# GroupNorm with 4 MiB tiles: the last store of each run issued in four gated quarters of 32 rows

## The chip, the core and the metric

The kernel runs on one core of a Trainium2 chip. The core has TensorE (PE), VectorE (DVE), ScalarE (ACT), GpSimd (POOL), and SyncE (SP), which here issues all large transfers. Sixteen DMA engines move data between HBM and the on-chip memory SBUF, which has 128 rows (partitions). The metric is the device time of one execution in microseconds. All times below are of one core, so "slowest core" and "the core" are the same.

## The reference

The reference is a group normalisation of x, of shape (128, 1024, 32, 16) in bf16, with 32 groups of 32 channels. Each sample and group, 32 x 32 x 16 = 16,384 values, gets its mean and variance; the values are normalised and then scaled and shifted by channel.

```python
xr = x.reshape(B, G, C // G, H, W)
mu = xr.mean(axis=(2, 3, 4), keepdims=True)
var = ((xr - mu) ** 2).mean(axis=(2, 3, 4), keepdims=True)
xn = (xr - mu) / jnp.sqrt(var + 1e-5)
xn = xn.reshape(B, C, H, W)
return xn * g[None, :, None, None] + b[None, :, None, None]
```

The input has 134.2 MB and the output as much. Both pass through SBUF once.

## The kernel before

One tile holds four samples: 4 x 32 groups fill the 128 SBUF rows, and one row holds the 16,384 values of its group, 32 KB. A tile has 4 MiB, and there are NT = 32 tiles. NBUF = 6 buffers `xt[0..5]` hold tile i in buffer i % 6, and the result replaces the input in place.

For a tile, PE multiplies 32 slices of 512 columns by an identity and accumulates them in one PSUM bank (line 142). DVE sums that bank to the negative mean (line 161). ACT squares the difference from the mean in two halves with a running sum (line 255), and two small operations make the standard deviation (lines 269 and 276). DVE takes the reciprocal, makes scale and bias for each of the 32 channels of a row (lines 174 to 184), and rewrites the tile in 32 slices (line 194). `s_dve` counts finished tiles.

All tile transfers are issued by SP, in the order in which `sync_program` writes them, and each goes to the rings of the DMA engines in that order. First come the loads of tiles 0 to 5 (line 113). Then, for each tile, SP waits until DVE has finished it and issues its store (line 120). After every third store (RUN = 3; the tiles 1, 4, 7, ... 25 and, with no loads left to issue, 28 and 31) SP issues a run of up to three loads. Each of these first waits on `st[j]`, until the store that frees its buffer has landed. `load(8)`, `load(9)` and `load(10)`, for instance, follow the store of tile 4 and wait for the stores of tiles 2, 3 and 4. So the transfers come in runs: three stores, three loads, three stores, and so on.

A transfer's semaphore rises by 16 when it has landed, by one for each of the 16 DMA engines. `ld[j]` and `st[j]` are the semaphores of a buffer's loads and stores. A run's third load waits for the run's last store; the first two wait for earlier stores. At the end, line 295 waits for all stores.

Of the kernel before, what the change touches and what calls it, by code (L numbers as in the profile page):

```python
# [17 lines left out]
NBUF = 6  # L18
RUN = 3
# [5 lines left out]
def kernel(  # L25
# [8 lines left out]
    P = nc.NUM_PARTITIONS  # L34
# [6 lines left out]
    NT = B0 // NS  # L41
# [8 lines left out]
    o_v = out.rearrange("(t n) (g k) h w -> t (n g) (k h w)", n=NS, g=G)  # L50
# [6 lines left out]
    xt = [sb.tile([P, F], BF16, name=f"xt{j}") for j in range(NBUF)]  # L57
# [19 lines left out]
    def sem(name):  # L77
        return tc.alloc_semaphore(name)

    ld = [sem(f"ld{j}") for j in range(NBUF)]  # L80
    st = [sem(f"st{j}") for j in range(NBUF)]
    s_gb, s_set, s_eye, s_rep = sem("s_gb"), sem("s_set"), sem("s_eye"), sem("s_rep")
    s_pe, s_mean, s_sq, s_std = sem("s_pe"), sem("s_mean"), sem("s_sq"), sem("s_std")
    s_dd, s_dve = sem("s_dd"), sem("s_dve")
# [23 lines left out]
    def sync_program(sync):  # L108
        def load(i):
            j = i % NBUF  # L110
            if i >= NBUF:
                sync.wait_ge(st[j], 16 * (i // NBUF))
            sync.dma_start(out=xt[j][:], in_=x_v[i]).then_inc(ld[j], 16)

        for i in range(min(NBUF, NT)):
            load(i)
        for i in range(NT):
            j = i % NBUF
            sync.wait_ge(s_dve, i + 1)
            sync.dma_start(out=o_v[i], in_=xt[j][:]).then_inc(st[j], 16)  # L120
            if (NT - NBUF - 1 - i) % RUN == 0:
                for n in range(max(NBUF, i + 1 + NBUF - RUN), min(i + 1 + NBUF, NT)):
                    load(n)
# [162 lines left out]
    with tc.tile_critical():  # L286
        with nc.Block() as block:
            block.sync(sync_program)
            block.tensor(tensor_program)
            block.vector(vector_program)  # L290
            block.gpsimd(pool_program)
            block.scalar(scalar_program)

        for j in range(NBUF):
            nc.sync.wait_ge(st[j], 16 * len(range(j, NT, NBUF)))
# [30 lines left out]
```

## Time and profile before

| | |
|---|---|
| median of three runs | 633.49 us (633.39 to 634.88) |
| profiled execution | 632.89 us, span 631.1 us |
| ACT busy | 476.2 us, 75% |
| DVE busy | 375.6 us, 60% |
| PE busy | 260.1 us, 41% |
| data queue of the tile transfers | 9,216 packets, 268.44 MB, 99.0% of 16 engines' span |
| HBM read and written | 134.22 MB each, 425 GB/s over the span |
| load, from issue to landing | 29.1 us median, 32 loads of 4 MiB |
| store, from issue to landing | 33.3 us median, 32 stores of 4 MiB |

The span runs from the first to the last instruction; the time of the execution is some 1.8 us more. Issuing a transfer and waiting for a semaphore do not count as busy. The time from issue to landing contains the time in which a transfer stands in the rings behind earlier ones. The trace also has a record of each DMA packet: when it started, how long it took, and its size. A packet of a tile transfer is one row of 32 KB, and each of the 16 engines ends its share of a transfer with a 4-byte packet, called the completion packet below.

### The profile page before, as it was taken

The numbers are of one execution on the slowest core, as the hardware profiler recorded it, in microseconds if no ns is written. First come the engines' busy times: TensorE is split into PE (matmuls) and PEld (weight loads), VectorE is DVE, ScalarE is ACT, GpSimd is POOL, SyncE is SP. The second block draws the span as 40 slices with busy tenths as digits, with TensorE's granted clock in tenths as the row PEclk, the third lists the DMA queues.
The fourth block names the chain that finished last, engine by engine and source line by source line (L and its number), as shares of the span: only waits on it lengthen the run. The fifth ranks groups of instructions, "written<-read, shape, count | busy, mean of one in ns | idle before, by whom it ended". The sixth has DMA issues, their size and how long they took to land. (4 is left out here: it accounts for less than half of the span.)

```text
span 631.1 us, 3670 instructions
## 1 busy us (share of the span) xinstructions
PE 260.1 (41%) x1025; PEld 106.2 (17%) x1025; DVE 375.6 (60%) x1188; ACT 476.2 (75%) x194; POOL 0.9 (0%) x7
## 2 busy tenths in 40 slices
PE   1877409008602750572087018604720670095000
PEld 0333103003201310230032003201310230032000
DVE  0067477774772777077627745770777177447771
ACT  0596999996994699199819965993899199749940
POOL 0000000000000000000000000000000000000000
PEclk9988858658855975687578659755975796588555
DMA  8999999999999999999999999999999999999996
GB/s 366 431 432 402 434 434 432 435 432 432 430 432 434 434 432 434 432 432 434 432 432 430 432 434 430 432 434 432 426 436 434 434 428 434 432 436 432 432 397 287
DMA packets 9320, 268.53 MB, mean 425 GB/s; under 512 B 1120, under 2 KB 1120, under 8 KB 1120
## 3 DMA queue, kind: packets, MB, share of 16 engines
q1 hardware_dynamic: 9216, 268.44, 99.0%
q14 instruction: 6, 0.05, 0.0%
q8 instruction: 2, 0.03, 0.0%
q10 hardware_dynamic: 96, 0.00, 0.0%
HBM read 134.22 MB, written 134.22 MB: 425 GB/s over the span
## 5 line engine op out<-in xcount | busy, mean ns | idle before, releaser
L255 ACT ACTIVATE ja<-xt,negmean 128x8192 fp8e5<-128x8192 bf16 x64 | 455.5, 7117 | 127.1 <-DVE jd L161 120.6
L142 PE MATMUL pa<-xt,eye 128*128 128x512 bf16 x1024 | 259.9, 419 | 309.1 <-PEq L140 306.9
L194 DVE TENSOR_SCALAR xt<-xt,scl,bia 128x512 bf16<-128x512 bf16 x1024 | 333.6, 405 | 1.2
L142 PEld LDWEIGHTS pa<-xt,eye 128*128 128x128 bf16 x1024 | 106.1, 106 | 462.5 <-issue 368.8
L161 DVE TENSOR_SCALAR_CACHE_REDUCE jd<-pa 128x512 bf16<-128x512 f32 x33 | 22.6, 685 | 144.6 <-PE pa L142 142.8
L174 DVE RECIPROCAL rstd<-std 128x1 f32<-128x1 f32 x32 | 5.2, 162 | 82.9 <-ACT std L276 82.9
L255 ACT ACTIVATION_READ_ACCUMULATOR ja<-xt,negmean 128x1 f32 x64 | 11.9, 186 | 0.0
L276 ACT ACTIVATE std<-sq,half 128x1 f32<-128x1 f32 x32 | 9.4, 294 | 1.0
L269 ACT ACTIVATE half<-sq,eps_t 128x1 f32<-128x1 f32 x32 | 8.9, 278 | 0.0
L184 DVE SCALAR_TENSOR_TENSOR bia<-scl,negmean,gb 128x32 f32<-128x32 f32 x32 | 8.0, 251 | 1.1
L177 DVE TENSOR_SCALAR scl<-gb,rstd 128x32 f32<-128x32 f32 x32 | 7.7, 242 | 1.1
L157 DVE COPY gb<-gb_p 128x64 f32<-128x64 f32 x1 | 0.2, 225 | 9.8 <-PE gb_p L128 9.8
L128 PE MATMUL gb_p<-gb_b,rep 32*128 32x64 bf16 x1 | 0.2, 231 | 10.8 <-DMA gb_b<-in_b_dram 10.8
L250 ACT ACT_TABLE_LOAD x1 | 1.3, 1283 | 1.9 <-issue 1.9
L161 DVE DVE_READ_ACCUMULATOR jd<-pa 128x1 f32 x33 | 2.7, 81 | 0.0
L128 PEld LDWEIGHTS gb_p<-gb_b,rep 32*128 32x128 bf16 x1 | 0.1, 100 | 10.8 <-DMA gb_b<-in_b_dram 10.8
L156 DVE MEMSET ones_b<- 128x128 bf16 x1 | 0.2, 165 | 1.1 <-SPq L286 1.1
L229 POOL TENSOR_SCALAR_AFFINE_SELECT rep<-ones_b 32x128 bf16<-32x128 bf16 x1 | 0.3, 305 | 0.0
L220 POOL TENSOR_SCALAR_AFFINE_SELECT eye<-ones_b 128x128 bf16<-128x128 bf16 x1 | 0.3, 294 | 0.8 <-DVE ones_b L156 0.8
L250 ACT ACTIVATE warm<-eps_t 128x1 f32<-128x1 f32 x1 | 0.2, 203 | 0.0
L238 POOL TENSOR_SCALAR eps_t<-ones_b 128x1 f32<-128x1 bf16 x1 | 0.2, 204 | 0.0
L310 POOL MEMSET const-bfloat16-1.0<- 128x1 bf16 x1 | 0.1, 102 | 0.0
(3 smaller groups left out, 0.3 us busy)
## 6 DMA issues: line engine op xcount, KB each, us to landing
xt<-in_x_dram SPq DMA_DIRECT2D x32, 4096.0 KB, 29.1
out_dram<-xt SPq DMA_DIRECT2D x32, 4096.0 KB, 33.3
gb_b<-in_g_dram ACTq DMA_DIRECT2D x1, 2.0 KB, 6.1
gb_b<-in_b_dram ACTq DMA_DIRECT2D x1, 2.0 KB, 9.3
```

The source lines that it names most:

```text
L128: pe.matmul(out=gb_p[:].rearrange("p a k -> p (a k)"), lhsT=rep[:], rhs=gb_b[:].rearrange("q a k -> q (a k)"), start=True, stop=True,).the ...
L142: m = pe.matmul(out=pa[j][:], lhsT=eye[:], rhs=xt[j][:, k * MM_FREE : (k + 1) * MM_FREE], start=(k == 0), stop=(k == NMM - 1),)
L161: dve.tensor_scalar(out=jd[i % 2][:], in0=pa[i % NBUF][:], scalar1=-inv_n, scalar2=None, op0=ALU.mult, op1=ALU.add, accum_out=col(negmean, i),
L174: dve.reciprocal(out=col(rstd, i), in_=col(std, i))._wait_ge(s_std, i + 1).then_inc(s_dd, 1)
L177: dve.tensor_scalar(out=scl[j][:], in0=gam, scalar1=col(rstd, i), scalar2=None, op0=ALU.mult,)._wait_ge(s_dd, 3 * i + 2).then_inc(s_dd, 1)
L184: dve.scalar_tensor_tensor(out=bia[j][:], in0=scl[j][:], scalar=col(negmean, i), in1=bet, op0=ALU.mult, op1=ALU.add,)._wait_ge(s_dd, 3 * i ...
L194: m = dve.tensor_scalar(out=span, in0=span, scalar1=scl[j][:, k : k + 1], scalar2=bia[j][:, k : k + 1], op0=ALU.mult, op1=ALU.add,)
L220: pool.affine_select(out=eye[:], in_=ones_b[:], pattern=[[-1, P]], compare_op=ALU.is_equal, fill=0.0, base=0, channel_multiplier=1,)._wait ...
L250: act.activation(out=warm[:], in_=eps_t[:], func=ACT.Sqrt)
L255: m = act.activation(out=ja[:], in_=xt[j][:, h * F // 2 : (h + 1) * F // 2], func=ACT.Square, bias=col(negmean, i), scale=1.0, accum_out=s ...
L269: act.activation(out=col(half, i), in_=sq[:, 2 * j : 2 * j + 1], func=ACT.Identity, bias=eps_t[:], scale=inv_n,)._wait_ge(s_sq, 3 * i + 1) ...
L276: act.activation(out=col(std, i), in_=sq[:, 2 * j + 1 : 2 * j + 2], func=ACT.Sqrt, bias=col(half, i), scale=inv_n,)._wait_ge(s_sq, 3 * i + ...
```

## The change

Nine of the 32 stores, of the tiles 1, 4, 7, ... 25, are each replaced by four stores of 32 rows (1 MiB): rows 0 to 31, 32 to 63, 64 to 95 and 96 to 127. These are the stores that are followed by loads. The first two quarters are issued together, the third when the first has landed on all DMA engines, and the fourth when the second has. Then SP waits for the third, and only then goes on to the loads of the run. Three new semaphores `qt` count the first three quarters; the fourth raises `st[j]`, as the whole store did. The other 23 stores, all loads and all computation are as they were.

```diff
+    qt = [sem(f"qt{c}") for c in range(3)]
...
+        def gated(i):
+            return i < NT - NBUF and (NT - NBUF - 1 - i) % RUN == 0
+
+        def store_in_quarters(i):
+            j = i % NBUF
+            q = P // 4
+            n = 16 * (gates[0] + 1)
+            gates[0] += 1
+            for c in range(4):
+                if c >= 2:
+                    sync.wait_ge(qt[c - 2], n)
+                rows = slice(c * q, (c + 1) * q)
+                sync.dma_start(out=o_v[i][rows], in_=xt[j][rows]).then_inc(
+                    qt[c] if c < 3 else st[j], 16
+                )
+            sync.wait_ge(qt[2], n)
+
+        gates = [0]
         for i in range(min(NBUF, NT)):
             load(i)
         for i in range(NT):
             j = i % NBUF
             sync.wait_ge(s_dve, i + 1)
-            sync.dma_start(out=o_v[i], in_=xt[j][:]).then_inc(st[j], 16)
+            if gated(i):
+                store_in_quarters(i)
+            else:
+                sync.dma_start(out=o_v[i], in_=xt[j][:]).then_inc(st[j], 16)
```

## The prediction

> **What bounds the kernel now.** I read the page first: span, engines, slices, DMA part.
>
> ```profile
> span 631.1 us, 3670 instructions
> PE 260.1 (41%) x1025; PEld 106.2 (17%) x1025; DVE 375.6 (60%) x1188; ACT 476.2 (75%) x194; POOL 0.9 (0%) x7
> ...
> DMA  8999999999999999999999999999999999999996
> GB/s 366 431 432 402 434 434 432 435 432 432 430 432 434 434 432 434 432 432 434 432 432 430 432 434 430 432 434 432 426 436 434 434 428 434 432 436 432 432 397 287
> ...
> q1 hardware_dynamic: 9216, 268.44, 99.0%
> ```
>
> No compute engine is above 75%, while the one data queue (q1) is at 99%. In most slices it moves 430 to 436 GB/s, about 27 GB/s for each of 16 engines. Only the first slice and the last two are clearly lower.
>
> Next the waits and the timeline of the issuing queue (start, length, engine, line).
>
> ```profile
> SPq L120 <- DVE xt L194: 368.3, 23, 44.6
> SPq L113 <- DMA out_dram<-xt: 223.3, 25, 10.1
> ...
> 171.69 19.64 SPq L113 DMA_DIRECT2D xt<-in_x_dram  x3
> 191.38 30.22 SPq L120 DMA_DIRECT2D out_dram<-xt  x3
> 229.80 19.65 SPq L113 DMA_DIRECT2D xt<-in_x_dram  x3
> 249.50 30.17 SPq L120 DMA_DIRECT2D out_dram<-xt  x3
> ```
>
> SP waits, but DMA work does not run out: three loads are issued over 19.7 us, each when one more store has landed, while two 4 MiB transfers (19.4 us) still stand in the rings. So a change has to be priced in time of the DMA engines.
>
> Then the end: the chain that ended last, and two stretches of it (length, busy time by engine, clock, DMA share, GB/s).
>
> ```profile
> 551.87 0.04 issue
> 551.91 8.83 PE pa L142 x32
> ...
> 607.00 10.42 DVE xt L194 x32
> ```
>
> ```profile
> 613.70:618.20 4.50, 0.00 (x0) 0.00 (x0) 3.72 (x12) 0.00 (x0) 0.00 (x0) 0.50 0.27 117
> 618.30:628.90 10.60, 0.00 (x0) 0.00 (x0) 0.00 (x0) 0.00 (x0) 0.00 (x0) 0.50 0.88 377
> ```
>
> The chain begins at 551.9 us, when the load of tile 29 has landed: the packet records put that load's completion packets at 545.95 us on the first engine and 551.41 on the last. From there three tiles are computed until 617.4, then the last store. Whatever delays tile 29 delays the end by as much; all nine gated stores (tiles 1, 4, ... 25) lie before it.
>
> Last, the packet records. A data packet is one 32 KB row. Its 5th percentile and median are 1.213 us, its 95th 1.219, and it is the same in a load and a store. A 4 MiB transfer gives each engine 8 rows, 9.68 us. 64 transfers make 512 rows, 622 us with the small gaps of some 3 ns, of the 628.9 us at which the last packet ends. The stretch at 613.7 says more: a share of 0.27 is 4.3 engines, and 117 GB/s over these is again 27 GB/s each. An engine is no faster with most others idle. The limit is thus private to an engine or to the path it uses, and not a pool that all share.
>
> **The change, part by part.** The sum is made against the profiled execution: 632.9 us, of which 631.1 is the span and 1.8 lies around it. The median of the runs, 633.49, is 0.6 above that.
>
> Removed: nine whole stores, 8 rows for each engine, 9 x 9.70 us of ring time. Added: 36 stores of 32 rows and 27 waits. The bytes, the packets of data and all compute stay. Two engine orders matter.
>
> *The waits.* From a completion packet to work at an engine takes two steps. The last completion packet of the store that frees tile 11's buffer is at 171.21 us and SP issues the load at 171.69, so 0.48; the last store is issued at 617.44 and its first packet starts at 618.27, so 0.83. Together 1.31 us. While quarter n+2 is fetched so, quarter n+1 is in the rings: two rows an engine, 2.43 us at the present rate. So the handover is covered with 1.1 us to spare, and more if rows get slower. If that cover were gone, the two uncovered handovers per gate would cost at most 2 x 1.31 x 9 = 24 us.
>
> Behind the waiting SP stand the loads of the next run and then the next stores. The first two loads used to be issued while the gated store was still queued (171.69 and 181.35); now they come after the third quarter has landed. They were to run behind that store in the same rings anyway, and the fourth quarter covers the 1.31 us. The third load waits for the fourth quarter as it waited for the whole store, with two loads in the rings. The next stores come after it as now. In the steady periods their tiles are ready earlier (the store at 191.38 goes out right behind the loads), so nothing new waits there. The 27 extra issues, 0.34 us each by the timeline, fall where SP waits. Taken: 0.
>
> *The rows of a quarter.* A whole store reads all 128 SBUF rows at once, a quarter 32 neighbours. No transfer of that size with 32 rows is in the trace, so its rate has to be bounded. Low end: the 1.213 us belong to the engine; a quarter is two rows, 2.43 us, and four are what the store was. High end: they belong to a path that serves a fixed block of 8 neighbouring rows, 16 paths in all; then 32 rows lie behind four paths, a row takes 4.85 us, a quarter 9.70, a gate 38.8 and the nine gates cost 9 x 29.1 = 262 us more. I take the middle in ratio, two engines on one path: 2.43 us a row, 4.85 a quarter, 19.4 a gate, +9.70 us for each of nine gates, +87.3. That the paths are the limit I read from two rows: loads and stores have the same duration although they use HBM in opposite directions, so what holds them is what they share on the SBUF side; and the 27 GB/s stay when the others idle, as a fixed link would have it.
>
> [...]
>
> *The lag of engines.* By the completion packets one engine is 2.3 us behind the first at 73 us, 3.05 at 249, and 5.46 from 512 on. Four steps (+0.8 at 278, +0.8 at 395, +0.35 at 449, +0.45 at 507) come where the load run turns to stores. In a gate with shared paths a late engine loses nothing: its partner has used the path alone in the meantime, and the path's total is fixed. So the gates swallow the lag, and tile 29 arrives as for the early engines: -5.46, with about 0.5 left: -5.0. Added packets (27 completion packets an engine, below 20 ns each): +0.5.
>
> Sum: 632.9 + 87.3 - 5.0 + 0.5 = 715.7; with the 0.6 to the median, 716.
>
> **Rivals.**
>
> *The rate is the engine's own (A).* For it: nothing in the trace has two engines on one path. Against: the equal times of load and store. Then the waits are covered, and the steps at the turns to stores, 2.4 us in all, shrink since the engines start a load run together. Time 631 to 633.5: no change, or faster. This ends on the other side; it decides if a row of a quarter stays at 1.213 us.
>
> *Only eight engines get a quarter (B).* If a transfer's rows are tied to engines by their place, quarters 0 and 1 go to one half of the engines and 2 and 3 to the other, four rows a quarter, 4.85 us. For it: each engine does eight rows in a whole store. Against: the diff asks for 16 completions, which is no proof either way. The second half begins at 4.85 + 1.31 = 6.2 us and ends at 15.9; the first is done at 9.70 and gets loads when the third quarter has landed, 11.0 + 1.3 = 12.3. Loss 2.64 us a gate, 23.8 in all, plus the 3.5 by which the second half stays behind, less the lag of 5: about +22 to +27, time 656 to 661.
>
> *Blocks of neighbours (C).* Four engines on a path: +262, less the 5: about 890. For it only that it is the simplest layout.
>
> *The handover is slower than 1.31 us (D).* At low rate, each 1 us beyond 2.43 costs 2 us a gate, 18 us in all, decided where the store's completion takes over 1.1 us more than above. Time 634 to 658.
>
> **How the numbers follow.** Shared by two: 0.75. A: 0.12 (half of it faster by more than 0.3%, half within). B: 0.07. C: 0.03. D: 0.03. The shared case's own range is 705 to 728: the lag kept whole gives 721, 1% more for two engines in turn on a path 728; gates overlapping by a row at their borders (1.2 us each) 705. To hold 8 in 10 the range must reach down to B, 655; C and A stay out. About 0.3% is what a measurement of this kernel can tell from no change. Faster 0.06, same 0.06, slower 0.88.
>
> **What the profile after would show.** Right: packets of gated stores near 2.43 us, all others at 1.21; lower GB/s in the slices that hold a gate, with the DMA share still near full; the median time to landing of a quarter around 10 us; the stretch from the first load issue of one run to the next near 68 us instead of 58.4; the chain of the end starting near 634 with the same 66 us up to the last store's issue. Wrong: all packets at 1.21 us and a period of 58 (A); DMA share at a half in gates and four rows an engine (B); idle rings between quarters with rows at 1.21 (D). Also wrong would be compute at the head of the chain in mid-run, which I exclude: three tiles take 44.6 us of ACT in a period of 58 or more.

## The result and the profile after

The changed kernel takes 724.75 us (median of six, 723.22 to 725.33), the kernel before 633.92 on the same chip: a ratio of 1.1428, with a 95% interval of 1.1412 to 1.1444. The profiled execution after is one of 723.22 us with a span of 721.5, against 632.89 and 631.1 before; the difference of the spans is 90.4 us. Ratios and intervals leave out executions over 1.5% longer than the fastest of their kernel, while medians keep them: 638.85 us for rows 0 to 63, 707.67 and 728.92 for the quarters without waits (for which there is no ratio), 895.55 for the other order and 1408.41 for the single gate.

The page of the changed kernel, with the same parts as shown of before:

```profile
span 721.5 us, 3706 instructions
PE 265.9 (37%) x1025; PEld 107.6 (15%) x1025; DVE 375.8 (52%) x1188; ACT 476.2 (66%) x194; POOL 0.9 (0%) x7
...
DMA  9999999999999999999999999999999999999997
GB/s 376 435 432 404 242 409 398 271 334 409 431 276 376 405 436 222 427 403 391 269 431 420 320 302 436 401 309 342 425 432 234 387 414 421 225 416 432 436 431 327
...
q1 hardware_dynamic: 9648, 268.44, 98.4%
...
out_dram<-xt SPq DMA_DIRECT2D x36, 1024.0 KB, 12.2
```

The bytes and the busy times of the compute engines are those of before, but for PE (265.9 us and not 260.1). The DMA engines are as busy as ever, 98.4% against 99.0%, and yet in some slices they move half as much: 222 to 342 GB/s where it was 430 to 436. The work is the same, so it is the packets that are slower (2.55 us against 1.213 for a row, below). The 9,648 packets are 8,192 rows and 91 transfers x 16 completion packets, so each quarter ends with a completion packet on all 16 engines. The last line is the quarters: 12.2 us from issue to landing.

The waits of SP and its timeline (line 130 is a quarter, 114 a load, 144 a whole store):

```profile
SPq L130 <- DVE xt L218: 246.9, 9, 32.5
SPq L130 <- DMA out_dram<-xt: 221.1, 18, 24.3
SPq L144 <- DVE xt L218: 128.2, 6, 44.8
SPq L114 <- DMA out_dram<-xt: 57.6, 18, 4.8
```

```profile
284.96 4.04 SPq L114 DMA_DIRECT2D xt<-in_x_dram  x3
289.05 1.01 SPq L144 DMA_DIRECT2D out_dram<-xt  x2
320.32 26.38 SPq L130 DMA_DIRECT2D out_dram<-xt  x4
351.54 4.65 SPq L114 DMA_DIRECT2D xt<-in_x_dram  x3
```

From one run's first load to the next's it is now 66.6 us here and 68.5 in the mean, against 58.2. The three loads go out within 4 to 5 us and not over 19.7. One gate in a window of its own (columns as before: length, engines, clock, DMA share, GB/s):

```profile
203.07:220.74 17.67, 0.00 (x0) 0.00 (x0) 11.08 (x35) 16.33 (x10) 0.00 (x0) 0.50 0.98 237
```

Four mebibytes took 17.67 us at 237 GB/s with the engines 98% busy. The chain that ended last starts 90.6 us later and then has the same steps:

```profile
642.52 0.04 issue
642.56 9.64 PE pa L166 x32
...
698.45 10.42 DVE xt L218 x32
```

So everything was lost before tile 29 landed. The completion packets say where. For each transfer I take the mean time of its 16 completion packets, and then the difference from the transfer before it in the rings; the table has the mean over the eight steady periods (gates of tiles 4 to 25), in us. The runs e1, e4 and e7 are described below.

| | store | store | last store of the run | load | load | load | period |
|---|---|---|---|---|---|---|---|
| before | 9.69 | 9.69 | 9.69 | 9.68 | 9.68 | 9.77 | 58.2 |
| after | 9.69 | 9.66 | 17.96 | 11.07 | 9.68 | 10.47 | 68.5 |
| e1, columns | 9.69 | 9.69 | 9.86 | 10.32 | 9.68 | 10.56 | 59.8 |
| e4, rows 32 to 95 | 9.69 | 9.69 | 4.98 | 9.69 | 9.68 | 9.88 | 53.6 |
| e7, order 0 2 1 3 | 9.69 | 9.65 | 15.84 | 11.63 | 9.68 | 10.08 | 66.6 |

The gate costs 8.27 us more, the run's first load 1.39 and its third 0.70. Eight such periods make 82.6 us, the first gate (17.7 us, at tile 1) and the two loads behind it 10.0, and that is the 92.6 us by which tile 29 lands later in the mean of the engines. On the last engine it is 90.6, since that one is now 1.8 us behind the mean and not 3.8.

The packets agree. Of the 8,192 rows, 755 take over 2.3 us, with a median of 2.55 us, 2.1 times 1.213; before there were seven. The nine gates hold 1,152 rows, so about a third of those were faster: the gate's 17.96 us for eight rows are 2.24 us a row. All rows together took 709.0 us an engine against 624.1, 84.9 more. The rest of the 92.6, some 8 us, is time in which engines stood idle.

### The profile page after: what moved, and what is told of

It is laid out like the page before. It is cut to its first block, busy times and chain, and to the rows that moved or that the text cites. A ratio compares the mean times of both kernels' runs of the same rounds, so it can differ in the third digit from the quotient of the medians.

```text
span 721.5 us, 3706 instructions
## 1 busy us (share of the span) xinstructions
PE 265.9 (37%) x1025; PEld 107.6 (15%) x1025; DVE 375.8 (52%) x1188; ACT 476.2 (66%) x194; POOL 0.9 (0%) x7
## 3 DMA queue, kind: packets, MB, share of 16 engines
q1 hardware_dynamic: 9648, 268.44, 98.4%
## 5 line engine op out<-in xcount | busy, mean ns | idle before, releaser
L166 PE MATMUL pa<-xt,eye 128*128 128x512 bf16 x1024 | 265.7, 425 | 393.4 <-PEq L164 391.1
## 6 DMA issues: line engine op xcount, KB each, us to landing
out_dram<-xt SPq DMA_DIRECT2D x36, 1024.0 KB, 12.2
```

The lines of the kernel that those rows point to most:

```text
L166: m = pe.matmul(out=pa[j][:], lhsT=eye[:], rhs=xt[j][:, k * MM_FREE : (k + 1) * MM_FREE], start=(k == 0), stop=(k == NMM - 1),)
```

## The experiments

**The place of the rows.** Theory, as in the prediction: the rate would be that of paths into SBUF which belong to blocks of rows, and 32 neighbours would reach half of them. Rival: the cutting, the waits, or having few rows, costs the time. Two runs cut the gated store in half by different rows, and leave out the other half of these nine tiles.

```diff
+            part = i < NT - NBUF and (NT - NBUF - 1 - i) % RUN == 0
+            rows = slice(0, 64) if part else slice(0, P)      # e4: slice(32, 96)
-            sync.dma_start(out=o_v[i], in_=xt[j][:]).then_inc(st[j], 16)
+            sync.dma_start(out=o_v[i][rows], in_=xt[j][rows]).then_inc(st[j], 16)
```

> The kernel before, but the nine gated stores write only rows 0 to 63 (the other half of these tiles is left out, 18.9 MB less). If the two engines of a pair share a path because of where the rows lie, these 4 rows an engine take 2.43 us each, as long as 8 rows of a whole store: 630 to 640 us, no gain from leaving half out. If the rate is set by the number of rows an engine has, 4 x 1.21 us are saved nine times: 588 to 594 us.

> As the run with rows 0 to 63, but the nine gated stores write rows 32 to 95: as many rows, as many bytes, half of them on either side of row 64. If the place of the rows decides, and rows below and above 64 use different paths, each engine has its path alone: 588 to 596 us. If any store of fewer than 128 rows runs at half rate, 630 to 640 us as with rows 0 to 63.

Measured: rows 0 to 63 take 625.58 us, a ratio of 0.9825 (0.9775 to 0.9874), with executions between 618.5 and 638.9. Rows 32 to 95 take 590.87 us, 0.9307 (0.9292 to 0.9322). A window of each over about a period, first rows 0 to 63, then rows 32 to 95:

```profile
170.00:230.00 60.00, 23.10 (x96) 9.61 (x96) 36.67 (x117) 46.09 (x19) 0.00 (x0) 0.72 1.00 399
216.00:274.00 58.00, 24.32 (x100) 9.90 (x98) 38.97 (x124) 48.30 (x19) 0.00 (x0) 0.74 1.01 433
```

With rows 32 to 95 the mean rate stays at 433 GB/s, and the table has 4.98 us for the half store, 4.85 in seven of eight periods: exactly half. Four rows of that run take over 2.3 us; with rows 0 to 63 it is 305, again with a median of 2.55. The same number of rows and bytes, two starts 32 rows apart, and 43 us saved or some 10. Both runs write each half tile as one contiguous 2 MiB of the output, so the HBM side does not set them apart. Of the two, the place in SBUF decides; the rival falls. That paths shared by two engines are the reason is a reading: no record names a path. The place is shown to decide for stores; no run here loads fewer than 128 rows.

Rows 0 to 63 were expected at 630 to 640. Only the profiled execution, 638.85 us, lies in it: its period of 58.4 us is that of whole stores, so leaving half out gained nothing there. The other three, 618.5 to 626.6 us, gained 8 to 16 us; they have no trace. In the one that was traced the first and the last engine's landing at a load's own semaphore are 11 to 21 us apart from the load of tile 11 on, and an engine whose partner is in another transfer would have the path to itself for a while. That this is what the faster executions gained by is not shown.

**All rows in each quarter.** The changed kernel with quarters cut along the columns:

```diff
-            q = P // 4
+            q = F // 4
...
-                rows = slice(c * q, (c + 1) * q)
-                sync.dma_start(out=o_v[i][rows], in_=xt[j][rows]).then_inc(
+                cols = slice(c * q, (c + 1) * q)
+                sync.dma_start(out=o_v[i][:, cols], in_=xt[j][:, cols]).then_inc(
```

> Quarters cut by columns: 128 rows by 4,096 values, 1 MiB each, with the same waits; only the rows that a quarter holds differ from the changed kernel. If the loss is that 32 neighbouring rows reach SBUF over half of the paths, it goes away: 629 to 635 us, and no packet of a gated store takes twice its time for its size. If the loss is the cutting and the waits themselves, the time stays at 715 to 726 us.

Measured: 645.17 us, 1.0171 (1.0157 to 1.0185). The page:

```profile
GB/s 367 445 426 403 390 418 409 418 414 440 407 426 420 420 430 420 426 416 419 419 442 391 423 425 424 426 422 424 403 426 416 438 405 420 425 438 407 432 440 336
...
out_dram<-xt SPq DMA_DIRECT2D x36, 1024.0 KB, 8.3
```

Eighty of the 91 us are gone with the same waits and the same sizes, and the gate is back at 9.86 us. No 8 KB packet of a quarter took more than 0.56 us, with a median of 0.309. But 11 us stay, which neither theory had. Hardly any of them lie in the steady gates: by the table they are 0.64 us at the first load and 0.79 at the third, with 0.17 in the gate. The DMA engines did not run dry in the gates but for some 1 us at the first, so the handover was covered as forecast.

**The waits.** Both forms of quarters without the waits inside and behind the gate:

```diff
-                if c >= 2:
-                    sync.wait_ge(qt[c - 2], n)
...
-            sync.wait_ge(qt[2], n)
... (in load)
+                if gated(i - NBUF):
+                    for c in range(3):
+                        sync.wait_ge(qt[c], 16 * gates[0])
```

> Quarters of 32 rows as in the changed kernel, but all four are issued at once and only the load that needs the buffer waits for them. If the rows cost the time, some 80 us of the 91 stay: 713 to 722 us, with packets of 2.43 us in the gates; what goes is the idle time of the engines, 0.3 to 1.2 us a period. If the waits cost it, the time falls to 634 us.

> Column quarters as in the run e1_columns, all four issued at once; only the load that needs the buffer waits for them. What is left against that run's 645 us is the cutting into packets of 8 KB: 72 rows an engine at 4 x 309 ns and not 1,213 ns, 1.7 us. If the waits, which bring the engines into step, cost the rest of the 11 us, then 634 to 637 us. If the cutting costs it, 643 to 646 us.

Measured: rows 704.49 us, the median of four executions between 695.89 and 728.92, which neither theory had; columns 638.01 us, 1.0067 (1.0054 to 1.0081). In rows the waits are thus worth about 20 of the 91 us, though the spread of the four makes that rough. In the profiled executions it is 21.9 us between the spans (699.6 and 721.5), about three times the idle time. What went is packet time: all rows took 680.2 us an engine against 709.0 with the waits, and 399 rows take over 2.3 us where it was 755.

By the landings at the loads' own semaphores, the first and the last engine are 14 to 24 us apart without the waits from the load of tile 8 on, and 1.7 to 3.8 with them. So tile 29 lands 35 us earlier in the mean of the engines but only 22 on the last, and PE has to wait for the last. A likely reading is that engines which share a path and are in different transfers disturb each other less. It is argued: a packet's record does not name its engine, and the run also issues the loads earlier.

In columns the waits cost 7 of the 11 us. Of the 4 that stay, 1.7 are the cutting into 8 KB packets as reckoned, and the engines are 7.6 us apart at tile 29 where it was 5.5 before.

**Which turn costs?** Three runs on the 11 us of the columns. The first (e6) is the kernel before with loads issued later, the second (e10) is e1 with only the first of its nine gates, the third (e11) is e1 with a last piece of half the columns.

```diff
e6:
             if (NT - NBUF - 1 - i) % RUN == 0:
+                if 0 < i < NT - NBUF:
+                    p = i - 1
+                    sync.wait_ge(st[p % NBUF], 16 * (p // NBUF + 1))
e10:
-            return i < NT - NBUF and (NT - NBUF - 1 - i) % RUN == 0
+            return i == 1
e11:
...
+            for c, (lo, hi) in enumerate(((0, q), (q, 2 * q), (2 * q, F))):
+                if c == 2:
+                    sync.wait_ge(qt[0], n)
...
+            sync.wait_ge(qt[1], n)
```

> The kernel before with whole stores; before the loads of a run SP also waits for the store before the last, so the run's first two loads are issued together and one transfer later, as in the changed kernel, but nothing brings the engines into step. If late loads by themselves make the turns dear (0.6 us at the run's first load and 0.8 at its third in the run e1_columns, nine runs), 640 to 647 us. If the engines have to be in step for that, 633 to 635 us, no change.

> The run e1_columns with only its first gate, at tile 1. It brings the engines into step once; after that nothing keeps them there. If being in step makes the turns dear, the next load-to-store turn shows it and later ones less, as the engines drift apart again: 634.5 to 637 us. If the turns stay dear without gates, 641 to 646 us as with nine of them.

> The run e1_columns with pieces of a quarter, a quarter and a half of the columns: the half is issued when the first quarter has landed, the loads when the second has. The engines are brought into step as before, but a load now reaches the rings some 3.5 us before it is due and not 1.1. If the 0.6 us at the run's first load is the start of a load with too short a notice, it goes, nine times: 638 to 641 us, and the first row of that load takes 1.21 us again. If it belongs to the turn from stores to loads itself, 643 to 646 us.

Measured: 633.55 us, 0.9999 (0.9990 to 1.0008); 635.97 us, 1.0026 (1.0014 to 1.0037); 642.85 us, 1.0131 (1.0108 to 1.0154). Late loads alone cost nothing, but these were not as late as the changed kernel's: the first load of a run is issued 5 to 7 us before the first engine's part of the store ahead of it lands, in e1 only 1.3 to 1.6 us before. Engines in step alone cost nothing either, as far as one period shows it: in e10 they are 0.9 us apart from 104 to 180 us, and the transfers there take 9.68 us each at every turn. Its gate and the two loads behind it take 3.1 us more, and no later turn is dear. I had expected the next turn to show it.

The 0.64 us at the first load is mostly the short notice: in e11, with 4.2 to 4.6 us of notice, the load takes 9.85 us and not 10.32. But the gate there takes 10.32 and not 9.86, so the time fell by only 2.3 us, less than forecast. The 0.79 us before the third load's end (the 16 slowest of the last rows of that load take 1.7 to 2.0 us in the mean) appears in every steady period of e1 and e11, and hardly at all in the gateless periods of before, e6 and e10 (1.2 to 1.5 us). Its cause stays open.

**Order and number of gates.**

```diff
e7:
-                rows = slice(c * q, (c + 1) * q)
+                r = (0, 2, 1, 3)[c]
+                rows = slice(r * q, (r + 1) * q)
e9:
-            return i < NT - NBUF and (NT - NBUF - 1 - i) % RUN == 0
+            return i == 13
```

> The changed kernel with its quarters in the order rows 0, 64, 32, 96, so that the two in flight lie on either side of row 64. If an engine works through its ring in order and the engines stay in step, all sixteen are in the same quarter most of the time and little changes: 705 to 726 us. If the rings let the two quarters run beside each other, the gates cost nothing and it is 633 to 650 us.

> The changed kernel with only one of its nine gates, the one at tile 13; the other stores are whole. If each gate has its own price, by the profile after 8.3 us in the gate and 2.1 us at the turns around it, less some lag of the engines that the gate takes in, the time is 641 to 645 us. If most of the 91 us is paid once, or builds up from gate to gate, it is below 638 or above 650 us.

Measured: 700.31 us, 1.1036 (1.1016 to 1.1056), and 642.92 us, 1.0132 (1.0110 to 1.0154). One gate costs 8.8 us, nine cost 91, or 10.1 each. In the mean of the engines the one gate delays tile 29 by 10.1 us, a ninth of the 92.6; the last engine is delayed by 8.7, since it is less far behind than before. So the price is paid per gate. The other order came out below its expected 705 to 726: there the gate takes 15.84 us and not 17.96. I read it as two quarters on different paths that run beside each other where engines have moved apart, more than I had allowed for, but far from fully.

**The end of the kernel.** Since column quarters move at nearly full rate (9.86 us a gate in e1 against 9.69 for a whole store), I tried them where nothing covers a store: at the last one, with no gate anywhere.

```diff
+                    if c < 3:
+                        sync.wait_ge(s_part, 3 * (TRIPS - 1) + c + 1)
+                    else:
+                        sync.wait_ge(s_dve, i + 1)
+                    cols = slice(c * q, (c + 1) * q)
+                    sync.dma_start(out=o_v[i][:, cols], in_=xt[j][:, cols]).then_inc(
+                        st[j] if c == 3 else s_last, 16
+                    )
... (DVE, after slices 8, 16 and 24)
+                if k in (7, 15, 23) and i == HEAD + NBUF - 1:
+                    m.then_inc(s_part, 1)
```

> The kernel before, nothing gated, but the very last store (tile 31) goes in four column quarters, each as soon as VectorE has finished its eight slices; the run e1_columns shows that column quarters move at nearly the full rate. The last store now starts when all 32 slices are done (10.4 us) and takes 9.7 us; the quarters start 7.8 us earlier and the last one takes 2.5 us, so the end comes about 7 us earlier: 626 to 628 us. If the late engine of the trace holds the last quarters back, 629 to 633 us.

Measured: 633.84 us, 1.0002 (0.9993 to 1.0011), no change. The windows of its end:

```profile
613.00:620.00 7.00, 0.00 (x0) 0.00 (x0) 5.65 (x18) 0.00 (x0) 0.00 (x0) 0.50 0.99 415
620.00:633.00 13.00, 0.00 (x0) 0.00 (x0) 0.00 (x0) 0.00 (x0) 0.00 (x0) 0.50 0.44 185
```

The rings are now full to 620 us (a DMA share of 0.99), where before they stood three quarters empty from 613.7 to 618.2 (0.27). But the completion packets of the last piece run from 624.5 to 630.1 us: most engines are done early, and the late one, 6.6 us behind the first at 610, ends the kernel. In the kernel before, the late engine used the idle time to catch up: it is 5.5 us behind at the store before the last and 0.8 at the last. So no version here that writes all rows beats the kernel before.

## Why the prediction was right, and where its sum was off

The forecast was 716 us, with 655 to 728 as the whole range and 705 to 728 for the likeliest case; 724.75 lies in both. The step that decided it is that the place of a quarter's rows makes a row take about twice as long. That is shown by the runs with rows 0 to 63 and 32 to 95 (305 rows over 2.3 us against 4), and by the columns (no 8 KB packet over 0.56 us). That two engines share one path there fits the 2.1 times, but no run shows it. From the trace before it was a choice in the middle between two bounds, which that trace could not settle. Case A (the rate is the engine's) would have left the rows at 1.213 us; 755 take 2.55 in the median. Case B is out by engines busy at 98% in the gates, where it needed a half. Case C would have needed 4.85 us a row.

That the total came so near is in part luck, since errors of opposite sign cancel in it. And the upper end, 728, puts 1% on the whole time, while by the prediction's own reading two engines share a path only in the nine gates: 1% of 175 us is 1.7 us, and that end would then be 723, below what was measured.

Point by point:

- *A quarter's row at 2.43 us.* The 755 slow rows have 2.55 as median, 5% more; over a whole gate it is 2.24 us a row.
- *19.4 us a gate, +87.3 in all.* Too much: 17.96 us, and 8 x 8.27 + 8.03 = 74.2 for nine. I put that down to quarters that overlap at their borders, since rows 32 to 95, those of the second and the third, run at the full rate in e4 (4.98 us for a half store) and engines are not quite in step (1.5 to 5.3 us apart at the steady gates' completion packets); the other order points the same way (15.84 us a gate). The range had that term with one row, 1.2 us; it was 1.4 us a gate.
- *The waits: "Taken: 0".* Nearly right as to idle engines: at most 1.2 us in 68 outside the first two gates, some 8 us in all. Wrong as to what the waits do: without them the rows are some 20 us faster by e2. And a gate leaves its mark on the turns behind it, which the sum had not at all: 1.39 us at the first load and 0.70 at the third, with the first gate's loads 18.7 us in all. Half of the first is also there with columns; the rest I put down to the fourth quarter's slow rows beside those of the load, which is argued and not shown.
- *The lag: -5.0.* Measured -2.0. The gates took in some of the lag of the late engine, but the first and the last engine are still 3.2 us apart at tile 29. Case A had the turns to stores grow cheaper with engines in step; they got dearer.
- *Added packets: +0.5.* Not told apart.
- *A reading.* The fourth slice, at 402 GB/s, is clearly lower too, not only the first and the last two. Nothing in the sum rests on it.

With these sizes, 74.2 + 18.7 - 0.3 (of the stores) = 92.6, less 2.0 of lag, is 90.6 against the 90.4 between the spans. The forecast's +82.8 was thus the sum of a term that was 13 us too large, one of 19 us that it had not, and a lag 3 us too favourable. What the profile after was to show, it shows: a period of 68.5 us, slices at about half rate, a full DMA share, and a chain whose steps behind tile 29 are the same, though it starts at 642.5 and not 634. A quarter lands in 12.2 us and not 10.

## What to carry to other kernels

DMA engines that were 98% busy moved 237 GB/s in a gate here, and 430 to 436 in most slices before: read the GB/s of the slice and the duration of one packet (2.55 us against 1.213 for a row) beside the share. Cut a transfer along the columns and keep all 128 rows in each piece: that cost 11 us here where rows cost 91. If rows have to be cut, stores of rows 32 to 95 moved at full rate here (433 GB/s over a period) and those of rows 0 to 63 did not (399 GB/s). In this kernel, whose DMA engines are 98 to 99% busy, waits between transfers had a price of their own (7 us with columns, about 20 with rows) although the engines were hardly seen idle (some 8 us with rows), and in a tail that looked idle (a DMA share of 0.27) the last engine caught up, from 5.5 us behind to 0.8.

## What the runs showed of the hardware that was not expected

- The 755 slow rows of the changed kernel take 2.55 us in the median, 5% more than twice 1.213.
- Nine row gates cost 91 us with waits and about 70 without (62 to 95 in four executions), though the same rows are written in the same quarters. Without waits the engines drift 14 to 24 us apart, and the last one gives back 13 of the 35 us that the mean engine gains by tile 29.
- Behind a column gate the slowest of the last rows of a run's last load take 1.7 to 2.0 us, 0.7 to 0.8 us a period. Neither late loads (e6) nor engines in step (e10) bring it about alone; the cause is open.
- A run's first load that is issued 1.3 to 1.6 us before the store ahead of it lands takes 0.64 us longer; with 4.2 to 4.6 us of notice it took 9.85 us and not 10.32.
